# A swap's transfers on two queues, and GpSimd's weight work moved behind the second norm

## The chip, the cores and the metric

The kernel runs on one core of a Trainium2 chip. The metric is the device time of one execution in microseconds; the time before is the median of three runs, 691.76 us (691.75 to 692.23).

A core has five engines, each with its own queue of instructions, worked off in order: TensorE (PE, matrix products; PEld is its weight load), VectorE (DVE), ScalarE (ACT), GpSimd (POOL) and SyncE (SP), which here only issues transfers (DMAs). ScalarE and GpSimd can issue transfers as well. Engines wait for each other by semaphores, and only where one needs what another has written, or has to overwrite what another still reads.

## The reference

The input has 2048 rows of 512 numbers. Two blocks with residuals follow each other:

```python
h  = x + A(layernorm(x))          # y = irfft(rfft(x) * rfft(K)) + x * D_skip, K from dt, A, C
h2 = h + B(layernorm(h))

def B(x):                          # rows x 512
    t  = gelu(layernorm(x) @ w1)   # 512 -> 512
    ts = t with its four column groups shifted by +1, -1, +2, -2 rows
    x1 = x + ts @ w2               # 512 -> 512
    return x1 + gelu(layernorm(x1) @ w3) @ w4   # 512 -> 1792 -> 512
```

All values are float32.

## The kernel before, in words

The first 300 us are the convolution (block A). The change lies in the second half, `mixer_phase` (block B), from some 340 us on.

**Groups.** The 2048 rows are sixteen tiles of 128 rows, in four groups of four tiles (512 rows). The first layer, `layer1(q, f)`, multiplies group q with one of four column groups f of w1; the second, `layer2(j)`, makes one tile j of 128 rows and needs tiles of neighbouring groups because of the shift. Groups come in the order 3, 0, 1, 2. The "third group" of the change is the one with q = 2, `third` in the code; its parts are named `xt20` to `xt23` in the profile.

**Three products for one.** Each float32 operand of a product is split into a high part (rounded) and a low part (operand minus high part), and a product is three matmuls: high with high, high with low, low with high. Of an operand `x` the profile shows `xh` and `xl`. High parts are casts on ScalarE. Low parts are subtractions on VectorE or GpSimd, with both inputs in SBUF. `gelu(b, name)` makes two gelus on ScalarE and one low part on VectorE (`h_0l` to `h_3l` are the low parts of the four f of a group). `layer1` and `layer2` take twelve matmuls for each bank of PSUM; four banks go round.

**Turning a group.** Layer products need the group with columns on partitions. `swap(x, t)` does this with four VectorE transposes of 32x32 blocks and sixteen transfers of 64 KB that exchange the blocks. They all are on SP's queue, except that `second` (the group before) uses SP and GpSimd in turn and `turn2(1)` uses SP and ScalarE. `parts` then makes the high part (ScalarE) and the low part (VectorE) of each of four pieces.

**The second norm.** `norm2(q)` follows the statistics of the four tiles of group q: eleven VectorE instructions on 128x4 elements (`qa`, `qb`, `qr`, `qo` in the profile) make scale and offset, then four activations normalize the tiles, on ScalarE except one of group 1, which is on VectorE. `turn2(q)` swaps the result, for layer three.

**Weights.** The third layer is computed with seven products instead of eight (a Winograd scheme), so its weights need sums: `sum3()` makes four GpSimd additions of 128x256 (`raws`). `load3(s)` splits those weights; `raw3(s)` and `raw4(s)` fetch the raw weights of step s with transfers on SP; `load4(s)` makes high parts (ScalarE) and low parts (GpSimd) of two 128x512 blocks of w4 (`cs0w` and `cs1w` for s = 0). The first reader of load4(0) is `layer4a(0)`, the accumulating products `acc`.

**Order.** There is no planner in this half: the order in which the Python code emits instructions is the order on TensorE, VectorE, ScalarE and GpSimd (`InOrder`). A transfer on SP that has to wait for a semaphore holds up those behind it. `residual(j)` is a GpSimd addition after each `layer2(j)`, and `first_splits`, between the transposes and the transfers of `turn2(1)`, casts on ScalarE and subtracts on GpSimd. The order around the change is written out in lines 1426 to 1442; the lines that the change edits are

```python
    third = swap(XQ[0], XQ[1])
    ...
    layer1(2, 0), turn2(0), layer1(2, 1), load4(0), raw4(1), layer1(2, 2), sum3(), layer1(2, 3), layer2(6)
    layer2(7), norm2(1)
```

Of the kernel before, what the change touches and what calls it, by code (L numbers as in the profile page):

```python
# [11 lines left out]
F32 = mybir.dt.float32  # L12
# [3 lines left out]
ALU = mybir.AluOpType  # L16
# [1112 lines left out]
def mixer_phase(ctx, tc, cst, h, out, finish, w3, w4):  # L1129

    nc = InOrder(tc)
# [13 lines left out]
    def slot(i):  # L1145
        return cst["slab"](i)
# [4 lines left out]
    XQ = [w1p.tile([128, 4 * 512], F32, name=f"xq{i}") for i in range(4)]  # L1151
# [5 lines left out]
    def bank(name):  # L1157
        return ps.tile([128, 512], F32, tag="bank", name=name)
# [11 lines left out]
    def gelu(b, name):  # L1170

        hi, lo, g = slab(f"{name}h"), slab(f"{name}l"), tmp(f"g{name}")
        nc.scalar.activation(hi, b, AF.Gelu_apprx_tanh)
        nc.scalar.activation(g, b, AF.Gelu_apprx_tanh)
        nc.vector.tensor_tensor(lo, g, hi.bitcast(F32), ALU.subtract)
        return hi, lo
# [37 lines left out]
    def norm1(q):  # L1214
        XL[q] = []
        for j in range(q * 4, q * 4 + 4):
            t = quarter(XQ[{3: 0, 0: 1, 1: 2, 2: 0}[q]], j % 4)
            if (q < 2 and j % 2) or (q == 3 and j != 14):
                nc.vector.tensor_scalar(t, h[:, j, :], mv[:, j, 0:1], r12[:, j : j + 1], ALU.subtract, ALU.mult)
            else:  # L1220
                nc.scalar.activation(t, h[:, j, :], AF.Identity, scale=r12[:, j : j + 1], bias=off12[:, j : j + 1])
            XL[q].append(t)
# [4 lines left out]
    def swap(x, t, order=range(4), queues=(nc.sync,), between=lambda: None):  # L1227

        blocks = t.rearrange("p (b c i t) -> p i c b t", b=4, c=4, i=4)
        for i in order:  # L1230
            nc.vector.transpose(blocks[:, i], quarter(x, i).rearrange("p (c b t) -> p c b t", c=4, b=4))
        between()
        for a in range(4):
            for b in range(4):
                queues[b % len(queues)].dma_start(quarter(x, a)[b * 32 : b * 32 + 32], quarter(t, b)[a * 32 : a * 32 + 32])
        return [turned(x)[:, c] for c in range(4)]
# [9 lines left out]
    def layer1(q, f):  # L1246
        b = bank(f"l1_{q}_{f}")
        n = 0
        seq = [(c, wi, xi) for c in range(4) for wi, xi in PROD]
        if (q, f) in ((3, 0), (1, 0)):  # L1250

            seq.sort(key=lambda k: 2 * k[0] + 3 * k[2])
        for c, wi, xi in seq:
            nc.tensor.matmul(b, W1[f][wi][:, c * 128 : c * 128 + 128], XT[q][c][xi], start=(n == 0), stop=(n == 11))
            n += 1
        H1[q, f] = gelu(b, f"h1_{q}_{f}")

        tiles = {0: ((15, 0),), 2: ((14, 1), (15, 2)), 1: ((0, 3),), 3: ((0, 4), (1, 5))}[f]
        for t, i in tiles:
            if t // 4 != q:  # L1260
                continue
            for k in range(2):
                src = H1[q, f][k][:, t % 4 * 128 : t % 4 * 128 + 128]
                dst = wrap[k][i // 4][:, i % 4, :]
                if f in (0, 2):
                    nc.gpsimd.tensor_copy(dst[:, 32:128], src[:, 0:96].bitcast(F32))
                    nc.gpsimd.tensor_copy(dst[:, 1:32], src[:, 96:127].bitcast(F32))
                    nc.gpsimd.tensor_copy(dst[:, 0:1], zero)
                else:
                    nc.gpsimd.tensor_copy(dst[:, 0:96], src[:, 32:128].bitcast(F32))  # L1270
                    nc.gpsimd.tensor_copy(dst[:, 96:127], src[:, 1:32].bitcast(F32))
                    nc.gpsimd.tensor_copy(dst[:, 127:128], zero)
# [3 lines left out]
    def h1_block(f, j, k):  # L1276
        if 0 <= j < 16:
            return H1[j // 4, f][k][:, j % 4 * 128 : j % 4 * 128 + 128]
        return wrap[k][WRAP[f, j] // 4][:, WRAP[f, j] % 4, :]
# [4 lines left out]
    def layer2(j):  # L1284
        q, i = divmod(j, 4)
        b = bank(f"l2_{j}")
        n = 0
        for f, sh in enumerate((-1, 1, -2, 2)):
            for wi, xi in PROD:
                nc.tensor.matmul(b, h1_block(f, j + sh, xi), W2[f][wi], start=(n == 0), stop=(n == 11))  # L1290
                n += 1
        x1 = quarter(X1[q], i)
        nc.vector.scalar_tensor_tensor(x1, h[:, j, :], r1[:, j : j + 1], b, ALU.mult, ALU.add)
        xq[j] = x1
        if j < 8:
            residual(j), stats2(j)

    def residual(j):
        (nc.gpsimd if j < 12 else nc.vector).tensor_tensor(h[:, j, :], h[:, j, :], xq[j], ALU.add)

    def stats2(j):
        q, i = divmod(j, 4)
        if q not in mv2:
            mv2[q] = sm.tile([128, 4, 2], F32, tag="mv2", name=f"mv2_{q}")
        st = sm.tile([128, 6], F32, tag="bst", name=f"st1_{j}")
        nc.vector.bn_stats(st, xq[j])
        nc.vector.bn_aggr(mv2[q][:, i, :], st)

    def norm2_ops(q):

        m = mv2[q]
        ra_, rb_, rs = (sm.tile([128, 4], F32, tag=f"q{i}", name=f"q{i}") for i in "abr")
        o = sm.tile([128, 4], F32, tag="qo", name="qo")
        ops = rsqrt_ops(nc, m[:, :, 1], EPS, rs, ra_, rb_)
        ops.append(lambda: nc.vector.scalar_tensor_tensor(o, m[:, :, 0], -1.0, rs, ALU.mult, ALU.mult))
        for i in range(4):
            x1 = xq[q * 4 + i]
            if (q, i) == (1, 3):
                ops.append(lambda: nc.vector.tensor_scalar(x1, x1, rs[:, 3:4], o[:, 3:4], ALU.mult, ALU.add))
            else:  # L1320
                ops.append(lambda i=i, x1=x1: nc.scalar.activation(x1, x1, AF.Identity, scale=rs[:, i : i + 1], bias=o[:, i : i + 1]))
        return ops

    def norm2(q):
        for op in norm2_ops(q):
            op()
# [4 lines left out]
    FT, XC, W3, W4 = {}, {}, {}, {}  # L1331

    def turn2(q, *how):

        for c, v in enumerate(swap(X1[q], XQ[{0: 2, 1: 0, 2: 3, 3: 1}[q]], *how)):
            FT[q, c] = v
# [31 lines left out]
    raw = {n: w1p.tile([128, k * 512], F32, name=f"raw{n}") for n, k in (("a", 1), ("b", 1), ("4", 1), ("5", 1), ("s", 2))}  # L1368

    def raw3(s):  # L1370
        f = s % half
        for i in range(2):
            o = (f + i * half) * 128
            nc.sync.dma_start(raw["ab"[i]].rearrange("p (c f) -> p c f", c=4),
                              w3[:, o : o + 128].rearrange("(c p) f -> p c f", p=128))

    def sum3():
        a11, a12, a21, a22 = (raw[n][:, i * 256 : i * 256 + 256] for n in "ab" for i in range(2))
        s1, s2, s3, s4 = (raw["s"][:, i * 256 : i * 256 + 256] for i in range(4))
        nc.gpsimd.tensor_tensor(s1, a21, a22, ALU.add)  # L1380
        nc.gpsimd.tensor_tensor(s3, a11, a21, ALU.subtract)
        nc.gpsimd.tensor_tensor(s2, s1, a11, ALU.subtract)
        nc.gpsimd.tensor_tensor(s4, a12, s2, ALU.subtract)
# [16 lines left out]
    def raw4(s):  # L1400
        for i in range(2):
            f = s % half + i * half
            nc.sync.dma_start(raw["45"[i]], w4[f * 128 : f * 128 + 128, :])

    def load4(s):
        W4[s] = []
        for i in range(2):
            o, r = (9 + i * 3 if s % 2 else i * 2), raw["45"[i]]
            nc.scalar.copy(slot(o), r)
            nc.gpsimd.tensor_tensor(slot(o + 1), r, slot(o).bitcast(F32), ALU.subtract)  # L1410
            W4[s].append((slot(o), slot(o + 1)))

    def slots(i, n):

# [11 lines left out]
    XT[1] = [parts(v, f"xt1{c}") for c, v in enumerate(second)]  # L1426
    root([2]), layer2(0), layer2(1)
    norm1(2), sum3()
    third = swap(XQ[0], XQ[1])
    layer1(1, 0), layer1(1, 1), layer1(1, 2), layer1(1, 3), load3(0), raw3(1)  # L1430
    layer2(2), layer2(3)
    XT[2] = [parts(v, f"xt2{c}") for c, v in enumerate(third)]
    norm2(0), layer2(4), layer2(5)
    layer1(2, 0), turn2(0), layer1(2, 1), load4(0), raw4(1), layer1(2, 2), sum3(), layer1(2, 3), layer2(6)
    layer2(7), norm2(1)

    def first_splits():
        for n in ("b11", "b21"):
# [115 lines left out]
    for s in range(2 * half):  # L1554
# [4 lines left out]
        if last:  # L1559
            load4(s)  # L1560
        else:
            load3(s + 1, *((nc.gpsimd,) if s else (nc.vector, (2,))))
# [20 lines left out]
        if not last and s:  # L1583
            load4(s), raw4(s + 1)
# [54 lines left out]
```

## Time and profile before

| | |
|---|---|
| median of three runs | 691.76 us (691.75 to 692.23) |
| profiled execution | 692.15 us, span 690.3 us |
| granted TensorE clock in it | 0.995 of full speed |
| TensorE busy | 651.8 us, 94% of the span |
| VectorE, ScalarE, GpSimd busy | 546.7, 407.8, 401.5 us |

The profile is of one execution. A row of its timeline has the start in us from the span's start, the duration in us, the engine, the line of the kernel (L87 is the helper that records all instructions of four engines, so rows are told apart by tile names), the operation, output and inputs by name with the numbers left out, and how many rows are merged (x4). In square brackets stands how long the engine stood idle before it and what ended that. SPq, ACTq and POOL rows with DMA_DIRECT2D are issues of transfers; the transfer itself lands later. A row of the list of waits has the engine that waits, the one waited for, the total in us, the number of times, and the longest.

### The profile page before, as it was taken

Reading aid. Unit: us, or ns where it says so; the run is one execution under the profiler, and the core shown is the slowest. Engines: PE = TensorE matmul, PEld = TensorE weight load, DVE = VectorE, ACT = ScalarE, POOL = GpSimd, SP = SyncE. Lnnn points to the kernel's source line nnn. Section 1 sums busy time; section 2 is a strip of 40 time slices with the busy share of each in tenths; the row PEclk is TensorE's granted clock in tenths of the full one; section 3 lists DMA queues with packets and bytes.
Section 4 is the critical chain, followed back from the end, with each engine's and each line's share of the span. In section 5 each row is a group of like instructions: output and inputs, shape, how many; then the busy total and the mean of one; then the engine's idle time right before and its main releaser. Section 6 shows DMA issues by size and latency. Waiting matters only on the chain.

```text
span 690.3 us, 16773 instructions
## 1 busy us (share of the span) xinstructions
PE 651.8 (94%) x6806; PEld 506.9 (73%) x6806; DVE 546.7 (79%) x960; ACT 407.8 (59%) x706; POOL 401.5 (58%) x414
## 2 busy tenths in 40 slices
PE   5887989999999997989999999999999999999997
PEld 5884756663677684848877888888888888888885
DVE  5998898999898998989868799766879954554554
ACT  7889878867889975245544445544465543444330
POOL 1889589967999998002556309455634555554310
PEclk9998999999999999999999999999999999999999
DMA  8840644011301133020232311233311342211004
GB/s 209 254 154 2 185 155 110 3 48 32 64 3 49 33 110 94 2 61 1 62 92 70 84 31 32 61 87 102 102 47 35 106 134 62 62 46 47 18 14 122
DMA packets 49393, 51.49 MB, mean 75 GB/s; under 512 B 6436, under 2 KB 33060, under 8 KB 49316
## 3 DMA queue, kind: packets, MB, share of 16 engines
q1 hardware_dynamic: 47908, 48.32, 24.8%
q10 hardware_dynamic: 1152, 1.57, 0.9%
q8 instruction: 53, 0.87, 0.5%
q0 software_dynamic: 256, 0.52, 0.3%
q14 instruction: 24, 0.20, 0.1%
HBM read 35.72 MB, written 8.39 MB: 64 GB/s over the span
## 4 chain that ended last, share of the span: by engine, by line
PE 57%; DVE 15%; ACT 12%; POOL 5%; DMA 4%; issue 4%; SPq 2%; ACTq 0%; DVEq 0%; POOLq 0%
PE l L87 20%; PE acc L87 11%; ACT pt L87 7%; PE bank L87 6%; DVE u L87 3%; DVE at L87 3%; PE l3e L87 3%; PE l3a L87 3%; PE l3c L87 3%; PE l3g L87 3%; PE l3f L87 3%; PE l3b L87 3%; PE l3d L87 3%; DVE cs L87 2%; DVE sn L87 2%
## 5 line engine op out<-in xcount | busy, mean ns | idle before, releaser
L87 ACT ACTIVATE pt<-pt 128x1056 f32<-128x1056 int32 x64 | 69.8, 1090 | 14.6 <-DVE cs L87 6.5
L87 POOL TENSOR_TENSOR pt<-p,s 128x512 int32<-128x512 int32 x64 | 71.9, 1140 | 5.2 <-DVE sn L87 4.2
L87 PE MATMUL bank<-at,tbs 128*64 128x128 f32 (+1 forms) x768 | 63.1, 311 | 3.3 <-DVE u L87 1.8
L87 PEld LDWEIGHTS bank<-at,tbs 128*64 128x64 f32 x768 | 44.7, 134 | 20.6 <-ACT at L87 3.0
L87 PEld LDWEIGHTS bank<-ident 128*128 128x128 f32 x418 | 50.8, 199 | 8.3 <-issue 5.1
L87 PE MATMUL bank<-ident 128*128 128x128 f32 x418 | 54.9, 288 | 0.0
L87 PE MATMUL bank<-u,ms 64*128 64x128 f32 x768 | 50.5, 280 | 3.4 <-DVE at L87 1.3
L87 PEld LDWEIGHTS bank<-u,ms 64*128 64x128 f32 x768 | 45.3, 188 | 8.2 <-issue 1.8
L87 POOL TENSOR_TENSOR cs0w<-raw,cs0w 128x512 fp32r<-128x512 f32 x7 | 9.1, 1295 | 59.0 <-ACT cs0w L87 47.4
L87 DVE TENSOR_TENSOR cs<-pt,amx 128x512 f32<-128x512 f32 x64 | 41.0, 679 | 2.4 <-ACT pt L87 1.3
L87 PEld LDWEIGHTS bank<-cs 128*32 128x32 f32 x1024 | 24.1, 111 | 22.9 <-POOL cs L87 6.1
L87 PE MATMUL bank<-cs 128*32 128x64 f32 x1024 | 32.6, 225 | 8.8 <-DVE cs L87 4.5
L87 POOL TENSOR_TENSOR sn1w<-raw,sn1w 128x512 fp32r<-128x512 f32 x7 | 9.5, 1359 | 53.3 <-ACT sn1w L87 42.9
L87 DVE TENSOR_TENSOR h<-h,l 128x512 f32<-128x512 f32 x48 | 32.0, 685 | 10.6 <-PE l L87 10.6
L87 DVE TENSOR_TENSOR u<-u,l3f 128x512 f32<-128x512 f32 x14 | 9.6, 683 | 36.9 <-PE l3f L87 36.9
L87 ACT COPY at<-bank 128x512 f32<-128x512 f32 x40 | 24.9, 629 | 22.9 <-PE bank L87 22.9
L87 ACT ACTIVATE pt<-pt,halfpi 128x1056 f32<-128x1056 f32 x32 | 38.0, 1188 | 0.5
L87 POOL TENSOR_TENSOR sn<-pt,amp 128x512 f32<-128x512 f32 x30 | 36.8, 1226 | 1.4 <-ACT pt L87 1.1
L87 DVE STREAM_TRANSPOSE at<-bank 128x512 f32<-128x512 f32 (+1 forms) x40 | 35.8, 927 | 1.9 <-PE bank L87 1.9
L87 ACT ACTIVATE u<-u 128x512 f32<-128x512 f32 x56 | 35.4, 632 | 1.8
L87 PE MATMUL bank<-sn 128*32 128x64 f32 x1024 | 32.0, 222 | 2.5 <-DVE sn L87 2.5
L87 POOL TENSOR_TENSOR cs<-pt,amp 128x512 f32<-128x512 f32 x26 | 31.9, 1226 | 3.5 <-PE bank L87 1.2
(1161 smaller groups left out, 2080.8 us busy)
## 6 DMA issues: line engine op xcount, KB each, us to landing
raw<-in_B_w_dram SPq DMA_DIRECT2D x28, 256.0 KB, 2.8
xq<-xq SPq DMA_DIRECT2D x80, 64.0 KB, 2.0
h<-in_A_u_dram SPq DMA_DIRECT2D x32, 128.0 KB, 4.3
h<-in_A_u_dram SPq DMA_DIRECT2D x16, 256.0 KB, 4.2
rawa<-in_B_w_dram SPq DMA_DIRECT2D x14, 256.0 KB, 2.9
rawb<-in_B_w_dram SPq DMA_DIRECT2D x14, 256.0 KB, 2.9
ms<-in_mm_dram SPq DMA_DIRECT2D x4, 768.0 KB, 11.2
out_dram<-h SPq DMA_DIRECT2D x48, 64.0 KB, 1.7
```

The lines of the kernel that those rows point to most:

```text
L87: ins = f(*args, **kw)
```

## The change

Three things change.

1. The sixteen transfers of the third group's swap go to SP's and GpSimd's queues in turn, eight each.
2. `load4(0)` is called with `later=True`: it makes only the two high parts, now after `layer1(2, 3)` and `layer2(6)`, and gives back a function that makes the two low parts.
3. That function (`low4`), `raw4(1)` and the second `sum3()` come after `norm2(1)` in the program. Before, `load4(0)`, `raw4(1)` and `sum3()` stood between the pieces of `layer1(2, ...)`.

By engine: TensorE and VectorE have the same order as before. On ScalarE the two high casts come after the gelus of `layer1(2, 2)` and `layer1(2, 3)`. On GpSimd eight transfer issues come between the first `sum3()` and the low parts of `load3(0)`, and the two low parts and four additions come after the residual additions of tiles 6 and 7. On SP `raw4(1)` comes after the sixteen transfers of `turn2(0)`.

```diff
-    def load4(s):
-        W4[s] = []
+    def load4(s, later=False):
+        at_ = [9 + i * 3 if s % 2 else i * 2 for i in range(2)]
+        W4[s] = [(slot(o), slot(o + 1)) for o in at_]
+
+        def low(i):
+            nc.gpsimd.tensor_tensor(W4[s][i][1], raw["45"[i]], W4[s][i][0].bitcast(F32), ALU.subtract)
+
         for i in range(2):
-            o, r = (9 + i * 3 if s % 2 else i * 2), raw["45"[i]]
-            nc.scalar.copy(slot(o), r)
-            nc.gpsimd.tensor_tensor(slot(o + 1), r, slot(o).bitcast(F32), ALU.subtract)
-            W4[s].append((slot(o), slot(o + 1)))
+            nc.scalar.copy(W4[s][i][0], raw["45"[i]])
+            if not later:
+                low(i)
+        return lambda: [low(i) for i in range(2)]
...
-    third = swap(XQ[0], XQ[1])
+    third = swap(XQ[0], XQ[1], queues=(nc.sync, nc.gpsimd))
...
-    layer1(2, 0), turn2(0), layer1(2, 1), load4(0), raw4(1), layer1(2, 2), sum3(), layer1(2, 3), layer2(6)
-    layer2(7), norm2(1)
+    layer1(2, 0), turn2(0), layer1(2, 1), layer1(2, 2), layer1(2, 3), layer2(6)
+    low4 = load4(0, True)
+    layer2(7), norm2(1), low4(), raw4(1), sum3()
```

## The prediction

> **What bounds the kernel now.** I read the page first, then the list of waits for TensorE over the mixer phase, then the windows, then the timelines of VectorE and GpSimd beside each other.
>
> ```profile
> span 690.3 us, 16773 instructions
> PE 651.8 (94%) x6806; PEld 506.9 (73%) x6806; DVE 546.7 (79%) x960; ACT 407.8 (59%) x706; POOL 401.5 (58%) x414
> ```
>
> TensorE (PE) is busy for 94% of the span. The list of its waits (total us, times, longest) from 300 to 410 us has two waits of the convolution's end and these three:
>
> ```profile
> PE l L87 <- DVE h_3l L87: 1.5, 1, 1.5
> ...
> PE l L87 <- ACT xt20h L87: 0.3, 1, 0.3
> PE l L87 <- DVE xt20l L87: 0.2, 1, 0.2
> ```
>
> These are the only places where TensorE stands in the stretch that the change touches, and both lie on it: the start of the third group's first layer (xt20) and the end of layer2(6) (h_3l). From there TensorE is solid, as the row of the windows view shows (us, then busy us of PE, PEld, DVE, ACT, POOL):
>
> ```profile
> 375.00:400.00 25.00, 25.00 (x112) 20.70 (x111) 18.54 (x38) 8.86 (x14) 8.47 (x8) 1.00 0.32 79
> ```
>
> So a gain can only come out of these stalls, and a loss must come from some other engine falling behind TensorE.
>
> **The change part by part. First, sixteen transfers over two queues.** Timeline rows (start, duration):
>
> ```profile
> 346.85 10.01 SPq L1235 DMA_DIRECT2D xq<-xq  x16
> ...
> 358.43 0.39 PE L87 MATMUL l<-ptw,h_3h 128*128 128x512 f32 x1
> 358.44 0.62 ACT L87 CAST xt20h<-xq 128x512 fp32r<-128x512 f32 x1 [7.72 <-DMA xq<-xq]
> 359.11 0.50 PE L87 MATMUL l<-xt20h,cs0w 128*128 128x512 f32 x1 [0.30 <-ACT xt20h L87]
> ...
> 362.50 0.39 PE L87 MATMUL l<-xt20h,cs0w 128*128 128x512 f32 x1
> ```
>
> SP issues sixteen in 10.01, so eight take 5.0 and end near 351.9. Matmuls of this shape stand 0.227 apart (from 362.50 here to 372.70 in the rows further down are 45 of them). Without a stall the twelve of layer1(2,0) would have ended at 358.43 + 13 x 0.227 = 361.38; they ended at 362.50. The whole loss is 1.12 us, more than the 0.5 that the waits list names, because the pipeline also refills. That is the upper bound of this part's gain.
>
> The other eight go to GpSimd. The second swap already has this form:
>
> ```profile
> 328.46 4.18 POOL L87 DMA_DIRECT2D xq<-xq  x8 [8.07 <-DVE xq L87]
> ...
> 335.90 0.62 ACT L87 CAST xt10h<-xq 128x512 fp32r<-128x512 f32 x1 [3.53 <-DMA xq<-xq]
> ```
>
> Eight issues cost GpSimd 4.18, and the cast came 3.26 after the last of them. GpSimd's queue around the third swap, and the last VectorE split of the group:
>
> ```profile
> 347.02 1.07 POOL L87 TENSOR_TENSOR raws<-rawa,raws 128x256 f32<-128x256 f32 x1
> 349.55 1.45 POOL L87 TENSOR_TENSOR w3s<-rawa,ptw 128x512 fp32r<-128x512 f32 x1 [1.47 <-ACT ptw L87]
> ...
> 354.00 2.54 POOL L87 TENSOR_TENSOR h<-h,xq 128x512 f32<-128x512 f32 x2
> ...
> 360.91 0.69 DVE L87 TENSOR_TENSOR xt23l<-xq,xt23h 128x512 fp32r<-128x512 f32 x1
> ```
>
> GpSimd is free at 348.09, issues until 352.3, and the cast of xt20h can come near 355.5, 2.9 earlier. But what is queued behind the issues moves too: load3(0)'s three low parts and two residual adds, 349.55 to 356.54 or 7.0 us, now run from 352.3 to 359.3. They were done before the splits xt20l to xt23l; now they run beside them, and both are two-operand SBUF instructions (below: they take turns). Interleaved, the work left over adds up: the splits begin at 356.1, wait for the rest of a weight part and for two adds of 1.25, and xt23l ends near 361.5, as before (361.60). TensorE gets xt20 and xt21 in time and waits a little for xt22l (about 361.0); layer1(2,0) ends near 362.15. Gain 0.35. Bounds: 1.12 if nothing collides; a loss of 0.5 if the issues or landings come half a us later, as the splits then end that much later. I take 0.35. raw3(1) on SP waits for the same low parts and so issues no earlier than now; the third layer, which reads load3(0), comes after all of layer two. Neither costs anything.
>
> **Second, sum3 and the low parts of load4(0) leave the place before h_3l.**
>
> ```profile
> 368.31 2.48 DVE L87 STREAM_TRANSPOSE xq<-xq 128x512 f32<-128x512 f32 x4
> ...
> 370.40 1.30 POOL L87 TENSOR_TENSOR cs1w<-raw,cs0w 128x512 fp32r<-128x512 f32 x1
> ...
> 370.71 1.53 DVE L87 TENSOR_TENSOR h_1l<-gh,h_1h 128x512 fp32r<-128x512 f32 x1
> ...
> 372.17 1.22 DVE L87 TENSOR_TENSOR h_2l<-gh,h_2h 128x512 fp32r<-128x512 f32 x1
> ...
> 372.50 10.01 SPq L1235 DMA_DIRECT2D xq<-xq  x16
> 372.70 0.39 PE L87 MATMUL l<-amp0w,h_3h 128*128 128x512 f32 x1
> ...
> 373.31 1.21 DVE L87 TENSOR_TENSOR h_3l<-gh,h_3h 128x512 fp32r<-128x512 f32 x1
> ...
> 374.58 0.50 PE L87 MATMUL l<-amp0w,h_3l 128*128 128x512 f32 x1 [1.49 <-DVE h_3l L87]
> ```
>
> and the same instruction in the group before, with GpSimd idle:
>
> ```profile
> 349.16 0.68 DVE L87 TENSOR_TENSOR h_3l<-gh,h_3h 128x512 fp32r<-128x512 f32 x1
> ```
>
> Each split was lengthened from 0.68 to 1.2 or 1.5 by GpSimd's additions. With GpSimd idle they step at 0.6: 370.71, 371.3, 371.9, and h_3l ends near 372.55, about when TensorE asks for it. The stall, 374.58 - 372.70 - 0.227 = 1.65 plus 0.1 of refill, goes: 1.75. Bounds 1.4 to 1.85. ScalarE's two high casts go behind the gelus, where ScalarE has nothing to do until the norm. Together with the first part, layer2(7) ends 2.1 earlier.
>
> SP's order changes as well: turn2(0)'s sixteen issues, whose transposes ended at 370.79 and which started at 372.50 behind raw4(1)'s wait for the low parts, come before it and start 1.7 earlier. Their first reader is a ScalarE cast that stands behind norm2(1)'s activations on its own engine, so nothing is gained. raw4(1) now goes out after the low parts, into an SP queue that is empty until turn2(1), and is not read before load4(1), behind the first two rounds of the third layer. Both cost nothing.
>
> **Third, where the moved work lands.** "Behind the second norm" is only the order on each engine: GpSimd waits for no norm. Its next instruction after residual(7) is the first low part, and six additions run while VectorE does norm2(1).
>
> ```profile
> 378.91 1.28 POOL L87 TENSOR_TENSOR h<-h,xq 128x512 f32<-128x512 f32 x1 [1.45 <-DVE xq L87]
> ...
> 379.81 0.41 DVE L87 TENSOR_SCALAR qa<-mv 128x4 f32<-128x4 f32 x1
> ...
> 382.04 0.16 DVE L87 SCALAR_TENSOR_TENSOR qo<-mv,qr 128x4 f32<-128x4 f32 x1
> ...
> 450.56 1.30 POOL L87 TENSOR_TENSOR cs0w<-raw,cs0w 128x512 fp32r<-128x512 f32 x1 [11.55 <-PE l L87]
> ...
> 455.28 0.73 POOL L87 TENSOR_TENSOR raws<-rawa,raws 128x256 f32<-128x256 f32 x1
> ```
>
> The norm is a chain of eleven tiny instructions, qa to qo. The first, qa, took 0.41 and ended at 380.22, just as the residual add did (380.19); the other ten then ran free in 1.98. So even 128x4 waits for a whole GpSimd addition. Two further rows agree, and the second pair tells who goes next:
>
> ```profile
> 459.78 0.59 DVE L87 TENSOR_SCALAR qb<-qa 128x4 int32<-128x4 int32 x1
> ...
> 255.12 0.45 DVE L87 TENSOR_TENSOR kt<-kt,dsk 128x16 f32<-128x16 f32 x1
> ...
> 254.01 1.51 POOL L87 TENSOR_TENSOR pt<-p,s 128x512 int32<-128x512 int32 x1
> ...
> 254.01 2.54 POOL L87 TENSOR_TENSOR pt<-p,s 128x512 int32<-128x512 int32 x2
> ```
>
> kt (16 elements) ended at 255.57, when the first of two back-to-back GpSimd instructions ended (255.52), and the second GpSimd instruction went on at once (2.54 for both). The h_1l rows show the same turns with longer instructions. So one tiny instruction passes at the end of each addition and the next waits for the following one. The same six additions stand undisturbed from 450.56 to 456.01: 5.45 us. Six of the ten pass by then; four more at 0.198 are done at 6.3 after qa, instead of 1.98. The chain becomes 4.3 longer. Bounds: 0 if tiny ones slip through, 5.45 if GpSimd keeps its turn to the end. I take 4.3, by the kt rows.
>
> The Trainium skill ("SBUF — State Buffer", section "Who interferes with whom") speaks against this placing: a VectorE instruction with two SBUF inputs contends with a GpSimd instruction that reads SBUF, and the second to issue fully blocks until the first finishes. The rows above agree that it is a full block; the page doesn't say whether a waiting VectorE instruction goes before GpSimd's next, and read as issue order alone it would make the chain 5.45 longer, which is a rival below.
>
> **Who waits for that.** Everything on VectorE behind norm2(1) is in order and follows without a break that could absorb it:
>
> ```profile
> 383.43 2.49 DVE L87 STREAM_TRANSPOSE xq<-xq 128x512 f32<-128x512 f32 x4
> ...
> 386.58 4.70 ACTq L87 DMA_DIRECT2D xq<-xq  x7
> ...
> 393.55 1.29 DVE L87 TENSOR_TENSOR t<-xq,xq 128x512 f32<-128x512 f32 x2
> ...
> 414.37 1.18 DVE L87 TENSOR_TENSOR h_010l<-u,h_010h 128x512 fp32r<-128x512 f32 x1 [0.17 <-ACT u L87]
> ...
> 415.60 0.50 PE L87 MATMUL acc<-cs0w,h_010l 128*128 128x512 f32 x1
> ```
>
> Norm, transposes, the issues that start as they end, the sums from 393.55, the splits up to h_010l: each starts when the one before ends. h_010l ended at 415.55 and TensorE took it at 415.60: 0.05 of slack. So the end moves with this chain, not with TensorE's own lead. The chain starts 2.1 earlier (it begins with layer2(7)) and is 4.3 longer: 2.2 later, less 0.05. TensorE first feels it at the third layer's first products, which read the splits of that chain. After 415.6 TensorE has no wait left that could give it back.
>
> **Sum.** -0.35 - 1.75 + 4.3 - 0.05 = +2.15. The profiled execution took 692.15 (span 690.3 and 1.85 around it), 0.39 above the median of 691.76. That makes 694.3 for such an execution and 693.9 for the median.
>
> **The rivals.**
> 1. Tiny instructions slip between or past GpSimd's additions, and the chain keeps its length. Then only the two gains are left: the chain comes 2.1 earlier, TensorE is nowhere stopped, 691.76 - 2.1 = 689.7, faster. For it: the data of a 128x4 instruction is nothing. Against: qa, qb and kt each waited to the end of the addition. It decides once the ten take under 2.7 from qa's end: then the chain is under 0.7 longer and more than 1.4 of the 2.1 is left.
> 2. Two pass per addition. The ten are done after the fifth end, about 4.95, so +3.0: 691.76 - 2.1 + 3.0 = 692.6, no change. The gaps between sum3's four instructions speak for it, as two of them depend on each other.
> 3. GpSimd keeps its turn (the issue-order reading), or the third group's splits collide worse and lose 0.5 instead of gaining 0.35: +5.45 - 2.1 or +2.15 + 0.85, 695.1 or 694.8.
>
> **How the numbers follow.** The forecast 0.62, rival 1 0.18, rival 2 0.12, rival 3 0.08. A measurement tells about 0.2%, or 1.4 us, from no change. Slower is the forecast and rival 3: 0.70; same is rival 2: 0.12; faster is rival 1: 0.18. The likeliest case alone has 693.2 to 695.1 (chain 3.6 to 5.5 longer). To leave out no more than 2 in 10 with its tails the range must reach rival 1: 689.6 to 695.4.
>
> **What would show it.** Right: SP's transfers of the third swap are eight in 5 us, with eight on GpSimd from 348.1; h_1l to h_3l near 0.68 each and no h_3l wait; the six additions of GpSimd beside norm2(1), whose instructions take up to 1.3 each, qo near 384.3; ScalarE's transfer issues near 388; TensorE waiting for b2200l, t200l or h_010l. Wrong: norm2(1) at 0.2 per instruction, or VectorE idle before the sums at 393 long enough to take the delay in.

## The result and the profile after

| | median | range | runs |
|---|---|---|---|
| before, run beside it | 692.17 us | 691.75 to 692.60 | 10 |
| changed kernel | 694.25 us | 693.21 to 694.37 | 10 |

The changed kernel is slower by 2.08 us; the ratio is 1.0026, with a 95% interval of 1.0016 to 1.0036. The granted clock was 0.995 in both profiled executions, so the clock plays no part. The head of the page of the changed kernel:

```profile
span 692.5 us, 16792 instructions
PE 651.7 (94%) x6806; PEld 505.8 (73%) x6806; DVE 551.3 (80%) x960; ACT 407.9 (59%) x706; POOL 403.0 (58%) x422
```

TensorE's work is the same (651.7 us against 651.8). VectorE is "busy" 4.6 us longer with as many instructions: an instruction that stands and waits for GpSimd counts as busy. The list of TensorE's waits from 300 to 430 us (total us, times, longest):

```profile
PE l3b L87 <- DVE t200l L87: 1.4, 1, 1.4
PE xt L87 <- ACT h L87: 1.0, 1, 1.0
PE bank L87 <- DVE at L87: 0.8, 1, 0.8
PE l3e L87 <- DVE u L87: 0.8, 1, 0.8
PE l3g L87 <- DVE b2200l L87: 0.5, 1, 0.5
PE l L87 <- DVE xt20l L87: 0.4, 1, 0.4
```

The wait of 1.5 us for `h_3l` is gone, and of the two waits at the third group's start one of 0.4 is left. In their place stand three waits of layer three, for `t200l`, `u` and `b2200l`: operands that VectorE makes behind the second norm. Now the third group, in the timeline (start, duration; in brackets the idle time before it and what ended it). SyncE and GpSimd each issue eight, and the split `xt20l` comes while GpSimd works off what queued up behind its issues:

```profile
347.18 4.96 SPq L1235 DMA_DIRECT2D xq<-xq  x8
348.36 3.93 POOL L87 DMA_DIRECT2D xq<-xq  x8
354.98 0.62 ACT L87 CAST xt20h<-xq 128x512 fp32r<-128x512 f32 x1 [3.91 <-DMA xq<-xq]
355.92 0.73 POOL L87 TENSOR_TENSOR w3s<-rawb,w3s 128x256 fp32r<-128x256 f32 x1
356.38 3.31 DVE L87 TENSOR_TENSOR xt20l<-xq,xt20h 128x512 fp32r<-128x512 f32 x1 [0.96 <-DMA rawa<-in_B_w_dram]
356.61 2.52 POOL L87 TENSOR_TENSOR h<-h,xq 128x512 f32<-128x512 f32 x2
359.75 0.50 PE L87 MATMUL l<-xt20l,cs0w 128*128 128x512 f32 x1 [0.39 <-DVE xt20l L87]
360.82 0.68 DVE L87 TENSOR_TENSOR xt23l<-xq,xt23h 128x512 fp32r<-128x512 f32 x1
...
362.40 0.39 PE L87 MATMUL l<-xt20h,cs0w 128*128 128x512 f32 x1
```

The cast of `xt20h` comes at 354.98 instead of 358.44, but `xt20l` stands for 3.31 us, to 0.56 behind the end of the second residual addition (359.13), so `xt23l` ends at 361.50, close to where it ended before. The last row is TensorE's first product of `layer1(2, 1)`; in the trace before it stands at 362.50. The three splits that GpSimd had lengthened are at their own length:

```profile
370.62 0.65 DVE L87 TENSOR_TENSOR h_1l<-gh,h_1h 128x512 fp32r<-128x512 f32 x1
371.19 0.68 DVE L87 TENSOR_TENSOR h_2l<-gh,h_2h 128x512 fp32r<-128x512 f32 x1
371.89 0.69 DVE L87 TENSOR_TENSOR h_3l<-gh,h_3h 128x512 fp32r<-128x512 f32 x1
```

And the second norm, VectorE's and GpSimd's rows together:

```profile
377.07 1.28 POOL L87 TENSOR_TENSOR h<-h,xq 128x512 f32<-128x512 f32 x1 [1.46 <-DVE xq L87]
377.97 0.41 DVE L87 TENSOR_SCALAR qa<-mv 128x4 f32<-128x4 f32 x1
378.31 1.30 POOL L87 TENSOR_TENSOR cs0w<-raw,cs0w 128x512 fp32r<-128x512 f32 x1
378.41 1.22 DVE L87 TENSOR_SCALAR qb<-qa 128x4 int32<-128x4 int32 x1
379.55 1.30 POOL L87 TENSOR_TENSOR cs1w<-raw,cs0w 128x512 fp32r<-128x512 f32 x1
379.67 1.21 DVE L87 TENSOR_SCALAR qr<-qb 128x4 int32<-128x4 int32 x1
380.79 0.75 POOL L87 TENSOR_TENSOR raws<-rawb 128x256 f32<-128x256 f32 x1
380.91 0.65 DVE L87 TENSOR_TENSOR qb<-qr 128x4 f32<-128x4 f32 x1
...
382.17 0.76 POOL L87 TENSOR_TENSOR raws<-raws,rawa 128x256 f32<-128x256 f32 x1
382.99 0.17 DVE L87 SCALAR_TENSOR_TENSOR qr<-qb,qr 128x4 f32<-128x4 f32 x1
383.01 0.74 POOL L87 TENSOR_TENSOR raws<-rawa,raws 128x256 f32<-128x256 f32 x1
383.19 0.59 DVE L87 TENSOR_TENSOR qb<-qr 128x4 f32<-128x4 f32 x1
...
384.21 0.16 DVE L87 SCALAR_TENSOR_TENSOR qo<-mv,qr 128x4 f32<-128x4 f32 x1
...
388.75 4.75 ACTq L87 DMA_DIRECT2D xq<-xq  x7
```

Each of the tiny instructions that are long ends 0.02 to 0.03 behind the end of a GpSimd addition (qb at 379.63, the addition at 379.61), and the next tiny one waits for the addition after it. What took 0.17 each takes 1.2 beside a low part and 0.65 beside a weight sum.

The traces differ by up to 2.3 us in when the second half begins, whatever the change, so I compare stretches, not clock times. For the two kernels and the first eight experiments, worked out from the timelines (us): from the start of `h_3l` of group 1 (ahead of the change) to the end of `xt23l`; from there to the end of `h_3l` of group 2; from there to the start of `qa`; from there to the end of `qo`; from there to the last instruction; and the sum.

| kernel | to xt23l | to h_3l | to qa | qa to qo | to the end | sum |
|---|---|---|---|---|---|---|
| before | 12.43 | 12.93 | 5.29 | 2.39 | 308.12 | 341.17 |
| changed | 12.01 | 11.08 | 5.39 | 6.41 | 308.17 | 343.05 |
| e1_queues_only | 12.00 | 12.91 | 5.29 | 2.39 | 308.03 | 340.62 |
| e2_move_only | 12.43 | 11.09 | 5.41 | 6.40 | 308.11 | 343.43 |
| e3_clear | 12.01 | 11.05 | 5.38 | 2.39 | 308.26 | 339.09 |
| e4_clear_one_queue | 12.44 | 11.05 | 5.41 | 2.38 | 308.14 | 339.42 |
| e5_lows_there | 12.01 | 11.09 | 5.38 | 4.48 | 308.27 | 341.23 |
| e6_sums_there | 12.02 | 11.09 | 5.41 | 4.30 | 308.23 | 341.05 |
| e7_blank | 12.04 | 11.03 | 5.41 | 2.97 | 308.17 | 339.61 |
| e8_adds_after | 9.53 | 12.85 | 5.36 | 2.40 | 308.16 | 338.29 |

The change is -0.42 - 1.85 + 0.10 + 4.02 + 0.05 = +1.90, against +1.88 from the sums (each entry is rounded) and +2.08 between the medians. Whatever delays or advances `qo` reaches the end whole: the last column stays within 0.24.

### The profile page after: what moved, and what is told of

Read it like the earlier page. It is cut to its first block, busy times and chain, and to the rows that moved or that the text cites. A ratio compares the mean times of both kernels' runs of the same rounds, so it can differ in the third digit from the quotient of the medians.

```text
span 692.5 us, 16792 instructions
## 1 busy us (share of the span) xinstructions
PE 651.7 (94%) x6806; PEld 505.8 (73%) x6806; DVE 551.3 (80%) x960; ACT 407.9 (59%) x706; POOL 403.0 (58%) x422
## 4 chain that ended last, share of the span: by engine, by line
PE 55%; DVE 19%; ACT 13%; issue 4%; POOL 4%; DMA 3%; SPq 1%; ACTq 1%; DVEq 0%; POOLq 0%
PE l L87 19%; PE acc L87 11%; ACT pt L87 8%; PE bank L87 6%; DVE u L87 4%; PE l3b L87 3%; PE l3d L87 3%; PE l3e L87 3%; PE l3a L87 3%; PE l3c L87 3%; DVE at L87 3%; PE l3g L87 3%; PE l3f L87 3%; DVE cs L87 2%; DVE sn L87 2%
```

## The experiments

Theory: each GpSimd addition beside the norm lets one tiny VectorE instruction through at its end, so the norm's chain is longer by what the additions there take, and the two gains ahead of it are real. Rivals: the delay has another cause (the casts, the issues, the position), or only the long additions hold the norm. Each ratio below is to executions of the kernel before that were taken beside the run (medians from 691.96 to 692.32 us).

### One part of the change alone

The two queues alone, on the kernel before:

```diff
-    third = swap(XQ[0], XQ[1])
+    third = swap(XQ[0], XQ[1], queues=(nc.sync, nc.gpsimd))
```

> The kernel before with only the third swap's sixteen transfers on two queues; low parts and sums stay where they were. Theory (GpSimd's additions take turns with norm2(1) and lengthen VectorE's chain by 4.3 us): the queues are nearly neutral, since xt23l ends where it did and h_3l is still late; 0 to -0.3 us against the kernel before. Rival (the loss comes from GpSimd issuing transfers and from the xt2 splits colliding with its residual additions): about +2 us. Rival (the transfers were the bottleneck): -1.1 us.

And the moved work alone, on the changed kernel:

```diff
-    third = swap(XQ[0], XQ[1], queues=(nc.sync, nc.gpsimd))
+    third = swap(XQ[0], XQ[1])
```

> The changed kernel with the third swap back on SP's queue alone; low parts and sums behind the second norm. Theory: the whole loss stays, norm2(1) takes 6.2 us instead of 2.2, h_3l's wait is gone; +2.0 to +2.5 us against the kernel before. Rival (the queues carry the loss): -1.7 us, from the h_3l wait alone.

With the queues alone 691.46 us (690.67 to 693.52), ratio 0.9992 (0.9983 to 1.0002): a gain of 0.5 that the times alone don't separate from none, but the first column of the table has it each time, 12.00 to 12.04 against 12.43 to 12.44. By the sums of the table it is 0.55, more than the 0 to 0.3 that was expected, because `xt23l` did not end where it had ended but 0.43 earlier. With the move alone 694.49 us (693.37 to 694.68), ratio 1.0033 (1.0020 to 1.0045). So the loss belongs to the move, and the queues give back a little.

### The moved work in clear places

The weight sums go beside `turn2(0)`'s transposes, which now come ahead of `layer1(2, 0)`, and the low parts go around `residual(6)`; nothing is left out. (`load4` now gives back `low` itself, so that the two low parts can stand apart; this holds for the experiments below as well, except for e7_blank.) The same with the third swap on SyncE alone is the fourth kernel.

```diff
-        return lambda: [low(i) for i in range(2)]
+        return low
...
-    layer1(2, 0), turn2(0), layer1(2, 1), layer1(2, 2), layer1(2, 3), layer2(6)
+    turn2(0), sum3(), layer1(2, 0), layer1(2, 1), layer1(2, 2), layer1(2, 3)
     low4 = load4(0, True)
-    layer2(7), norm2(1), low4(), raw4(1), sum3()
+    low4(0), layer2(6), low4(1), raw4(1), layer2(7), norm2(1)
```

> The changed kernel with the same six GpSimd additions put where VectorE runs no two-operand SBUF instruction that anyone waits for: sum3 during turn2(0)'s transposes (which go ahead of layer1(2,0)), one low part before and one after residual(6). Theory: norm2(1) is back at 2.2 us, h_1l to h_3l stay short, and the 2.1 us of stalls removed become a gain: -1.8 to -2.1 us against the kernel before, about 690.2. Rival (work is late because it is moved, or the lead of TensorE is worth nothing): no better than the kernel before.

> The same as e3_clear with the third swap on SP's queue alone. Theory: h_3l's stall alone is gained, -1.5 to -1.8 us against the kernel before; the difference to e3_clear is what the queues are worth once nothing else stands in the way, 0.2 to 0.4 us.

Measured: 689.96 us (689.30 to 690.28), ratio 0.9971 (0.9959 to 0.9983), and with one queue 690.28 us (689.63 to 691.53), ratio 0.9978 (0.9968 to 0.9988). The chain is back at its own length, 2.39, in the timeline of e3_clear:

```profile
377.67 0.41 DVE L87 TENSOR_SCALAR qa<-mv 128x4 f32<-128x4 f32 x1
378.12 0.17 DVE L87 TENSOR_SCALAR qb<-qa 128x4 int32<-128x4 int32 x1
...
379.90 0.16 DVE L87 SCALAR_TENSOR_TENSOR qo<-mv,qr 128x4 f32<-128x4 f32 x1
```

The same work with the same instruction count at another place in the order is worth 4.1 us (2.08 slower against 2.00 faster, each against the kernel before beside it; 3.96 by the sums of the table), and this version beats both kernels. The place is not wholly free: `h_1l` took 1.22 beside the last sum, but TensorE's list has no wait for it.

### The dose: half of the additions beside the norm

```diff
-    layer1(2, 0), turn2(0), layer1(2, 1), layer1(2, 2), layer1(2, 3), layer2(6)
+    turn2(0), sum3(), layer1(2, 0), layer1(2, 1), layer1(2, 2), layer1(2, 3)
+    layer2(6)
     low4 = load4(0, True)
-    layer2(7), norm2(1), low4(), raw4(1), sum3()
+    layer2(7), norm2(1), low4(0), low4(1), raw4(1)
```

> Only the two low parts stand in the second norm's window; the weight sums run earlier, beside the turn of the first quarter, where VectorE has transposes. Theory (each GpSimd addition lets one tiny instruction through at its end): two additions of 1.25 us each, so the chain from the start of qa to the end of qo is 4.4 to 4.6 us (2.39 in the kernel before, 6.40 in the changed one), only qb and qr are near 1.2 us, and the loss of +2.1 us eats the 2.1 us gained at h_3l and at the third group: 691.9 to 692.3 us, within 0.3 us of the kernel before. Rival (the norm's chain loses the same 4 us whatever stands beside it, because of the casts, the issues or the position): 693.8 to 694.3 us.

```diff
-    layer1(2, 0), turn2(0), layer1(2, 1), layer1(2, 2), layer1(2, 3), layer2(6)
+    layer1(2, 0), turn2(0), layer1(2, 1), layer1(2, 2), layer1(2, 3)
     low4 = load4(0, True)
-    layer2(7), norm2(1), low4(), raw4(1), sum3()
+    low4(0), layer2(6), low4(1), raw4(1), layer2(7), norm2(1), sum3()
```

> Only the four weight sums stand in the second norm's window; the low parts run earlier, around the residual additions. Theory: four additions of 0.69 us let four tiny instructions through, each near 0.66 us, and the other six are at 0.2 us: the chain from qa to qo is 4.4 to 4.7 us, and the time 691.9 to 692.4 us. With the run of the low parts alone the two losses add up to the 4.0 us that the changed kernel loses there. Rival (only the long additions of the low parts hold the chain, the short sums slip in between): 690.0 to 690.4 us.

Only the low parts: 692.15 us (691.29 to 693.55), ratio 0.9998 (0.9987 to 1.0010). Two tiny instructions are long, the third is not:

```profile
379.45 1.22 DVE L87 TENSOR_SCALAR qb<-qa 128x4 int32<-128x4 int32 x1
380.70 1.21 DVE L87 TENSOR_SCALAR qr<-qb 128x4 int32<-128x4 int32 x1
381.95 0.16 DVE L87 TENSOR_TENSOR qb<-qr 128x4 f32<-128x4 f32 x1
```

Only the sums: 692.07 us (691.01 to 695.48), ratio 1.0003 (0.9988 to 1.0017). Three are long at once, one slips through, one more is long:

```profile
377.28 0.66 DVE L87 TENSOR_SCALAR qb<-qa 128x4 int32<-128x4 int32 x1
...
379.36 0.16 DVE L87 SCALAR_TENSOR_TENSOR qb<-qb,qa 128x4 f32<-128x4 f32 x1
379.56 0.59 DVE L87 SCALAR_TENSOR_TENSOR qb<-qb 128x4 f32<-128x4 f32 x1
```

Against 2.39 the chains are 2.09 and 1.91 longer, together 4.00; in the changed kernel it is 4.02. The chain of the sums is 0.1 shorter than I had expected, by the one that slips through. The loss goes with the additions that stand there, and both kinds cost. The one that slips through (as `qr` at 382.99 in the changed kernel) starts in the gap ahead of the last sum, whose row starts 0.08 behind the end of the sum before it.

### Busy GpSimd, or GpSimd that reads?

The six additions of the changed kernel become GpSimd memsets of the same tiles, so this kernel leaves out two low parts and four weight sums:

```diff
-    def sum3():
+    def sum3(blank=False):
...
+        if blank:
+            for s_ in (s1, s3, s2, s4):
+                nc.gpsimd.memset(s_, 0.0)
+            return
...
-        return lambda: [low(i) for i in range(2)]
+        return lambda: [nc.gpsimd.memset(W4[s][i][1].bitcast(F32), 0.0) for i in range(2)]
...
-    layer2(7), norm2(1), low4(), raw4(1), sum3()
+    layer2(7), norm2(1), low4(), raw4(1), sum3(True)
```

> The changed kernel with its six additions in the second norm's window replaced by GpSimd clearing the same tiles: the low parts of two weight slabs and the second weight sums are left out, so this run measures the place and not the computation. Theory (what delays the norm is GpSimd reading two operands from SBUF, not that it is busy): the tiny instructions with two inputs stay at 0.16 to 0.17 us; the single-input qa, qb and qr are open, at most one clearing each: the chain is 2.4 to 4.4 us and the time 689.9 to 692.0 us, 690.0 the likeliest. By the Trainium skill's page SBUF - State Buffer, section Who interferes with whom, an operation of VectorE with two SBUF inputs does not meet a GpSimd operation that only writes. Rival (any work of GpSimd holds VectorE): one tiny instruction through per clearing, 693 to 694.5 us.

690.61 us (689.85 to 691.96), ratio 0.9979 (0.9967 to 0.9992). Timeline, GpSimd's memsets beside the norm:

```profile
378.85 0.55 POOL L87 MEMSET cs0w<- 128x512 f32 x1
378.97 0.46 DVE L87 TENSOR_SCALAR qb<-qa 128x4 int32<-128x4 int32 x1
...
379.84 1.09 POOL L87 MEMSET raws<- 128x256 f32 x4
379.95 0.16 DVE L87 TENSOR_TENSOR qb<-qr 128x4 f32<-128x4 f32 x1
380.14 0.16 DVE L87 SCALAR_TENSOR_TENSOR qb<-qb,qa 128x4 f32<-128x4 f32 x1
```

`qb` and `qr`, with one input, each wait for the end of a memset (0.46 instead of 0.17). Those with two inputs run at 0.16 while four memsets go on beside them. So it is not enough that GpSimd is busy; the kinds of the two instructions decide. The Trainium skill ("SBUF — State Buffer", section "Who interferes with whom") says that a VectorE instruction with two SBUF inputs meets a GpSimd instruction that reads SBUF and not one that only writes it, and that `tensor_scalar` (here `qb` and `qr`) can take the shared pair of ports, if its operands meet certain conditions. The rows of 0.16 agree with the first, and the waits of `qb` and `qr` fit the second; no run here shows whether their operands meet the conditions. The memsets are also shorter than the additions, so the time of this run measures the place with less work in it.

### Why did xt20l stand for three GpSimd instructions?

This I had not predicted: it should have passed at the end of the first. First, GpSimd's two residual additions are held back behind a one-element copy that needs `xt22l`, on e3_clear:

```diff
+            if j not in (2, 3):
+                residual(j)
...
     XT[2] = [parts(v, f"xt2{c}") for c, v in enumerate(third)]
+    nc.gpsimd.tensor_copy(sm.tile([128, 1], F32, tag="gate", name="gate"), XT[2][2][1][:, 0:1].bitcast(F32))
+    residual(2), residual(3)
```

> The variant with both parts of the moved work in clear places, and the residual additions of blocks 2 and 3 held back, by a one-element copy, until the third of the xt2 splits is done. In the changed kernel xt20l stood 3.31 us, through the last low part and both of these additions. Theory (it waits for GpSimd's additions and for nothing else): xt20l passes at the end of the last low part and takes 0.7 to 0.9 us, TensorE's wait of 0.4 us for it goes, and the time is 689.4 to 689.8 us, 0.2 to 0.6 below the variant without the hold. Rival (xt20l waits for something else that arrives near 359 us, such as its transfers): it still ends near 359.7, and the time is 689.9 to 690.3 us.

688.86 us (688.42 to 689.94), ratio 0.9951 (0.9933 to 0.9969): the fastest of all, and 0.5 below what I had expected. The timeline:

```profile
355.92 0.82 DVE L87 TENSOR_TENSOR xt20l<-xq,xt20h 128x512 fp32r<-128x512 f32 x1 [0.96 <-DMA rawa<-in_B_w_dram]
358.56 2.53 POOL L87 TENSOR_TENSOR h<-h,xq 128x512 f32<-128x512 f32 x2
358.67 1.21 DVE L87 TENSOR_SCALAR qb<-qa 128x4 int32<-128x4 int32 x1
```

`xt20l` passes in 0.82 and TensorE has no wait for it any more. The sum of the table falls by 0.80 against e3_clear, twice the wait of 0.4 that the list had named. A side effect, seen in the last two rows: the two additions now stand beside the first norm, where `qb` and `qr` take 1.21 each, one for each addition; its chain has room, and nobody waits. So it is GpSimd's additions that `xt20l` waits for, and the same two additions, one behind the other, do let a waiting instruction through at each end, here.

What is special about the place, then? Three runs on e3_clear. The semaphore waits ahead of `xt20l` are meant to move to a tiny copy of their own:

```diff
+    nc.vector.tensor_copy(sm.tile([128, 1], F32, tag="gate", name="gate"), third[0][:, 0, 0:1])
     XT[2] = [parts(v, f"xt2{c}") for c, v in enumerate(third)]
```

> The variant with both parts of the moved work in clear places, and in front of the xt2 splits a one-element VectorE copy that reads the transferred rows, so that the eight semaphore instructions that stand in front of xt20l stand in front of this copy instead. If those waits are what let GpSimd keep its turn, xt20l passes at the end of the GpSimd instruction that runs when it starts and takes 0.7 to 1.9 us, and the splits behind it take turns with the additions; their last end hardly moves, and the time is 689.2 to 690.0 us. Rival (the waits have nothing to do with it): xt20l stands 3.0 to 3.4 us again, through both additions, and the time is 689.8 to 690.4 us.

A tiny memset between GpSimd's last low part and the two additions:

```diff
     layer1(1, 0), layer1(1, 1), layer1(1, 2), layer1(1, 3), load3(0), raw3(1)
+    nc.gpsimd.memset(sm.tile([128, 4], F32, tag="gate", name="gate"), 0.0)
```

> The variant with both parts of the moved work in clear places, and between GpSimd's last low part of the third layer and its two residual additions the clearing of a tile of 128x4. If it is the order of GpSimd's instructions (additions back to back behind the low part) that keeps xt20l out, xt20l passes at the end of the low part, in 0.7 to 0.9 us, and xt21l shows the same thing once more: 1.2 to 1.8 us if a split can pass between the two additions, 2.9 to 3.2 us if it can't; the time is 689.2 to 690.0 us. Rival (it is xt20l itself, with its waits): xt20l stands 3.2 to 3.8 us as before, and the time is 689.8 to 690.4 us.

A one-element addition directly ahead of `xt20l`, in `parts`:

```diff
         nc.scalar.copy(natural(hi), src)
+        if name == "xt20":
+            one = hi[:, 0:1].bitcast(F32)
+            nc.vector.tensor_tensor(sm.tile([128, 1], F32, tag="gate", name="gate"), one, one, ALU.add)
```

> The variant with both parts of the moved work in clear places, and directly in front of xt20l a one-element VectorE addition that reads the cast xt20h. If the standing belongs to the place (any VectorE instruction with two SBUF inputs that arrives there waits for GpSimd's whole run), the tiny addition takes 2.4 to 3.4 us and xt20l behind it 0.7. If it belongs to xt20l (its size or its strided rows), the tiny addition passes at the end of the GpSimd instruction that runs, in under 1.5 us, and xt20l is long again, 2.4 to 3.4 us. Third way: the tiny addition passes at one end and xt20l at the next, both under 1.9 us. The time is 689.6 to 690.4 us by all three.

The first did not do what it was meant to do: `xt20l` still began only 0.82 behind the end of the copy, although its cast had ended with the copy at 354.70, so not all of the waits had gone to the copy, and `xt20l` stood for 3.31 again (690.40 us, 689.33 to 691.70, ratio 0.9975, 0.9965 to 0.9985). So this run says little of the waits. The second changed nothing: `xt20l` stood for 3.37, straight through the memset (690.13 us, 689.08 to 691.17, ratio 0.9974, 0.9961 to 0.9986). The third tells something; the time is 689.53 us (689.01 to 690.15), ratio 0.9969 (0.9949 to 0.9988), and the rows are

```profile
354.24 3.52 DVE L87 TENSOR_TENSOR gate<-xt20h 128x1 f32<-128x1 f32 x1 [0.17 <-ACT xt20h L87]
354.51 0.74 POOL L87 TENSOR_TENSOR w3s<-rawb,w3s 128x256 fp32r<-128x256 f32 x1
355.21 2.52 POOL L87 TENSOR_TENSOR h<-h,xq 128x512 f32<-128x512 f32 x2
357.68 0.68 DVE L87 TENSOR_TENSOR xt20l<-xq,xt20h 128x512 fp32r<-128x512 f32 x1
```

An addition of one element, with one wait, stood for 3.52 us, through four GpSimd instructions (it came while the second low part ran). So it is neither the size of `xt20l`, nor its rows, nor its waits: it is the place. One thing that this place has and the norm has not is that GpSimd's run follows on transfers that GpSimd issued, without an idle moment. The last run takes the issues away and keeps a run: the third swap on SyncE alone, and the first two low parts computed several times over, so that GpSimd is still at work when the splits come.

```diff
-            low.tensor_tensor(lo, src, hi.bitcast(F32), ALU.subtract)
+            for _ in range((2, 3, 1)[i] if s == 0 else 1):
+                low.tensor_tensor(lo, src, hi.bitcast(F32), ALU.subtract)
```

> The variant with both parts of the moved work in clear places and SyncE's queue alone, with GpSimd's first low part of the third layer's weights computed twice and the second three times (the same values), so that GpSimd again works through a run of additions when the splits arrive (to about 361.8 us), but issued no transfers ahead of it. If the transfers that GpSimd issued are what made it keep its turn, xt20l passes at the end of the instruction that runs, in 0.6 to 1.9 us, the splits take turns with the rest, and the time is 689.9 to 691.5 us. If a run of additions that was ready all along is enough, xt20l stands to the run's end, 2.5 to 4.5 us, TensorE waits for it 2 to 4 us, and the time is 692 to 694.5 us.

```profile
358.12 1.11 DVE L87 TENSOR_TENSOR xt20l<-xq,xt20h 128x512 fp32r<-128x512 f32 x1 [4.02 <-ACT xt20h L87]
359.15 1.22 DVE L87 TENSOR_TENSOR xt21l<-xq,xt21h 128x512 fp32r<-128x512 f32 x1
359.78 3.42 POOL L87 TENSOR_TENSOR h<-h,xq 128x512 f32<-128x512 f32 x2
360.29 1.77 DVE L87 TENSOR_TENSOR xt22l<-xq,xt22h 128x512 fp32r<-128x512 f32 x1
```

Here the splits and the additions take turns, one and one, as I had predicted for the changed kernel. The expectation bound a time to each outcome, and that was wrong: the turns came as in the first case, the time, 692.81 us (692.19 to 694.59), ratio 1.0015 (1.0001 to 1.0030), as in the second, because TensorE now waits for each of the four splits (0.2 to 0.7 us each).

## Why the prediction was right

The forecast was 693.9 us with "slower" the likeliest; 694.25 was measured, and by its own baseline +2.15 against +2.08. The signs, the places and the sizes held; one mechanism inside did not.

**The third group, -0.35.** Measured -0.43: `layer1(2, 1)` began 12.91 behind the start of group 1's `h_3l` (362.40 - 349.49), before 13.34 (362.50 - 349.16). Near in size, and wrong in the step "interleaved, the work left over adds up": nothing was interleaved. GpSimd kept its turn to the end of its run and the four splits came behind it. That `xt23l` was predicted near 361.5 and found at 361.50 is chance, since this trace runs 0.33 behind the one before; from `h_3l` on it ended 0.33 earlier than predicted (12.01 against 12.34), because GpSimd's run ended 0.50 earlier (9.64 against 10.14). The order changed who waits: TensorE stood 0.39 for `xt20l`, not a little for `xt22l`. So the size came out by another way than forecast, and that it is so near is in part luck. The issues were as forecast: eight in 4.96 on SyncE, eight on GpSimd from 348.36; they took 3.93 there and not 4.18, and the cast came at 354.98 against "near 355.5". The upper bound of this part was right: with the additions held back (e8_adds_after) `layer1(2, 1)` began at 12.20, a gain of 1.14 against the bound of 1.12.

**h_3l, -1.75.** Measured -1.85, and +0.10 from there to `qa`: -1.75. TensorE's rows agree: from the start of `layer1(2, 1)` to `qa` 17.31 before (379.81 - 362.50) and 15.57 after (377.97 - 362.40). The three splits took 0.65, 0.68 and 0.69, and the wait is gone.

**The norm's chain, +4.3.** Measured +4.02. One tiny instruction for each end, as read from the rows of `kt`; six additions of 5.44 (378.31 to 383.75). The forecast had six through by the last end and four behind it; it was seven and three, since `qr` at 382.99 slipped into the gap between the last two sums. That and the steps of 0.2 are the 0.28 too much. Rival 1 (tiny ones slip past) would need the ten to take under 2.7: they took 6.0. Rival 2 (two for each end) falls by every row; rival 3 (issue order to the end, +5.45) falls here, though at the third group GpSimd did what it says. The Trainium skill ("SBUF — State Buffer", section "Who interferes with whom") has the second to issue block until the first finishes: beside the norm the block is full, but for one addition only, and 4.02 is what that gives.

**Who waits, -0.05.** Between `qo` and the end the changed kernel differs by 0.05 and the others by at most 0.15; the 0.05 of slack is too small to be seen. From `h_3l` on, `qo` was forecast at 35.14 (384.3 - 349.16) and ended at 34.88 (384.37 - 349.49), and ScalarE's seven issues started 1.84 later than before. One reading was loose: VectorE does not work without a break there. Ahead of the sums it stood idle for 2.70 us before and for 4.59 after, until ScalarE's cast `cs1w` was done. The chain runs through ScalarE in that time (the seven issues to 393.50, then the cast to 394.59), so the idle time took nothing in, and the sums came 1.88 later (46.27 against 44.39 from `h_3l`). TensorE met the delay at `b2200l` (0.5), `t200l` (1.4) and `u` (0.8), two of them named ahead. That the chain has no reserve also works the other way: with the norm free the end came 2.08 earlier (e3_clear, by the sums).

## What to carry to other kernels

Behind another engine's step in program order is not after it in time: if the engine that gets the moved work has no reason to wait, it does the work beside that step. A VectorE instruction of 128x4 with inputs in SBUF waits for the end of the GpSimd addition that runs (here 0.65 to 1.22 us instead of 0.17), so keep GpSimd's additions and subtractions away from chains of tiny VectorE instructions that everything else waits for, and put them beside transposes, statistics or PSUM reads. (The four transposes took 2.46 beside the sums in e3_clear and 2.48 in the changed kernel with GpSimd idle; beside a residual addition in the changed kernel the statistics took 0.70 and a read of PSUM 0.72, elsewhere 0.69 and 0.75.) When a chain has no slack to the end, price a change by the stretches of that chain; here stretches that should be equal agreed to 0.1 us up to `qo`, and to 0.24 over the 308 us behind it, between traces whose clock times lay 2 us apart.

## What the runs showed of the hardware that was not expected

**GpSimd kept its turn behind transfers that it had issued.** In nine kernels GpSimd issued eight transfers and then ran without a pause through low parts and residual additions; in all nine the first VectorE instruction to come stood to the end of that run: `xt20l` for 3.29 to 3.37 us past two ends at which it could have gone (three in e10_gap, with the memset's), one element for 3.52 us past three. Without the issues (e12_late_no_issue), and with a pause behind them (e8_adds_after), a waiting instruction passed at each end. That points to the issues, and would fit a state that they leave and a pause clears; but one run without issues, in which the splits also came later, does not settle it, and why it is so stays open.

**Gaps of 0.1 us are used.** Where a GpSimd addition starts 0.08 behind the end of the one before it, a tiny VectorE instruction with two inputs started in the gap and took 0.16 or 0.17 (e6_sums_there and the changed kernel).

**A stall cost more than the wait that is listed.** The 0.4 of `xt20l` was worth 0.7 to the end of `h_3l` (22.38 against 23.06 from the table) when it went. The prediction had read the same from the trace before, where the two waits of 0.5 in all stood for 1.12.
